# Loading V in key blocks on SP instead of by head on GpSimd, with keys in natural order throughout

## Chip, core and metric

The kernel runs on one core of a Trainium2 chip. The metric is the device time of one execution in microseconds. Six runs of the kernel before have a median of 333.22 us (331.32 to 335.84).

## What is computed

Sliding-window attention over 8 batches of 8 heads, 576 positions and a head size of 64 (a key counts if it is at most 32 positions away), and then, on the 4,608 tokens of 512 features that the heads make side by side, a two-layer block with a squared relu.

```python
scores = scale * np.matmul(q, k.transpose(0, 1, 3, 2))
mask = np.abs(pos[:, None] - pos[None, :]) <= window
attn = softmax(np.where(mask, scores, -1e9))
out = np.matmul(attn, v)
x = out.transpose(0, 2, 1, 3).reshape(B * S, H * D)
h = x @ w_in
g = s * np.maximum(h, 0) ** 2 + b
result = g @ w_out
```

All inputs and the result are float32 in HBM. The kernel works in bfloat16 with float32 sums.

## The kernel before

Two heads make a pair, so there are four pairs. A batch has nine tiles of 64 keys and five units of up to 128 query rows, which lie 32 rows off the tiles. K of a pair is laid out block-diagonally (KBD: head 0 on partitions 0 to 63 and columns 0 to 63, head 1 on the other half of both), so one matmul scores 64 keys of both heads; keys of head 0 stand on the upper half of the score partitions, those of head 1 on the lower. V has the same form (VBD, two slots, one for even and one for odd batches): for a tile of 64 keys, head 0's rows lie on partitions 0 to 63, head 1's on 64 to 127, with two columns of ones for the row sums.

For a unit, TensorE makes the scores (L548) in PSUM (SC, two banks), ACT takes the exponential (L565), DVE multiplies by the 0/1 mask of the window (L571; for batch 0 TensorE adds a mask of large negative numbers instead, L554), TensorE multiplies by V (L588), DVE divides by the row sums (L598, L601), and the rows are transposed into XT, which the two-layer block reads: by TensorE and ACT for batches 0 to 2 (L610, L613), by a DMA transpose on SP after that (L618).

The two-layer block goes over blocks of tokens (128, 128, 256 and then 512). The first layer (function s1) has matmuls L702 into two PSUM banks W, a relu on ACT (L709) and a square on DVE (L711). The second layer (s2) has matmuls L721 into two banks O, an eviction with scale and offset on DVE (L734) and a store on SP (L738). The offset needs column sums of w_out: two sets of 16 matmuls (L744, function colsum), one for each half of w_out's columns.

Loads: q and k come in chunks of 256, 256 and 64 positions with all heads, issued by SP, cast to bfloat16 and transposed (batches 0 and 1: TensorE, L478; from batch 2 on: a DMA transpose on SP, L519, and then for K four DVE copies into KBD, L526). Weights come in 512 KB pieces (L417) and are cast by POOL, ACT or DVE (L420). V comes by head into a single float32 buffer VST and is cast into VBD by four instructions (cast_v, L450 on ACT, L451 on the others). For batches 0 and 1 SP issues eight transfers of 147 KB, one for each head (L437). From batch 2 on POOL issues sixteen transfers of 74 KB, two for each head: positions with an even number go to one 32-partition group, odd ones to the next. With that, the keys of a tile stand evens first, then odds, in V and K from batch 2 on, and the plain K copies L526 write 32 neighbouring columns; for batches 0 and 1 keys are in natural order and the K copies from PSUM (L495, L496) write every second column. So there are two masks: MASKH for natural order and MASK (four equal copies) for evens first.

What orders the work: each instruction is a task with a cost, a key and its data dependences, and a planner builds five queues (TensorE, ACT, DVE, POOL, SP) by simulating them: the task that can start first goes next, and the key decides between equals. Every queue is in order on the chip, so a waiting instruction holds all behind it. Keys count up from −200 for the start-up loads (nxt) and come from the due time of a unit after that. Loads of q and k from batch 2 on wait for an earlier unit's V matmuls (PACE, through paced), and so do those of V (PACEV). A slack tells the planner to plan a reader later than the landing it expects: 3,000 ns for V casts of batches 2 to 7.

Of the kernel before, what the change touches and what calls it, by code (L numbers as in the profile page):

```python
# [22 lines left out]
PACE = ((0, 0, 1, 2, 3, 3), (0, 0, 1, 2, 3, 3), (0, 1, 2, 3, 3, 3))  # L23
PACEV = ((0, 0, 1, 1), (0, 0, 1, 1), (0, 1, 2, 2))
# [4 lines left out]
class _Task:  # L29
    __slots__ = ("n", "stream", "fns", "cost", "lat", "key", "deps", "users", "left",  # L30
                 "ready", "start", "fin", "dma", "sem", "seq", "val", "used", "snap", "slack")

    def __init__(self, n, stream, fns, cost, lat, key, dma, slack):
        self.slack = slack
        self.n, self.stream, self.fns, self.cost, self.lat, self.key, self.dma = \
            n, stream, fns, cost, lat, key, dma
        self.deps, self.users = set(), []
        self.ready = self.start = self.fin = 0.0
        self.sem = self.seq = self.val = None
        self.used = False  # L40
        self.snap = None


class _Graph:
# [7 lines left out]
    def __init__(self, queues):  # L52
        self.queues = queues
        self.tasks = []
        self.writer, self.readers = {}, {}

    def add(self, stream, fns, cost, reads=(), writes=(), key=0.0, accum=False, dma=None, waits=(),
            lat=None, slack=0.0):
        if not isinstance(fns, list):
            fns = [fns]  # L60
        t = _Task(len(self.tasks), stream, fns, cost, self.LAT[stream] if lat is None else lat, key,
                  dma, slack)
        t.deps.update(waits)
        for r in reads:
            assert r in self.writer, r
            t.deps.add(self.writer[r])
        for w in writes:
            if w in self.writer:
                t.deps.add(self.writer[w])
            if not accum:  # L70
                t.deps.update(self.readers.get(w, ()))
        t.deps.discard(t)
        for r in reads:
            self.readers.setdefault(r, []).append(t)
        for w in writes:
            self.writer[w] = t
            if not accum:
                self.readers[w] = []
        self.tasks.append(t)
        return t  # L80
# [33 lines left out]
    def _order(self):  # L114
        free = {s: 600.0 for s in self.STREAMS}
        for t in self.tasks:
            t.left = len(t.deps)
            t.users, t.ready = [], 0.0
# [5 lines left out]
        while len(order) < len(self.tasks):  # L124
            best = None
            for s in self.STREAMS:
                for t in open_[s]:
                    c = (max(free[s], t.ready), t.key, t.n)
                    if best is None or c < best[0]:
                        best = (c, t)  # L130
            assert best is not None, "a cycle"
            (st, _, _), t = best
            open_[t.stream].remove(t)
            t.start = st
            free[t.stream] = st + t.cost
            t.fin = st + t.cost
            if t.dma is not None:
                t.fin = st + self.land.get(t.n, t.cost + 1800.0 + t.dma[1] * t.dma[2])
            order.append(t)
            for u in t.users:  # L140
                u.left -= 1
                if u.stream == "pe" and t.stream == "pe":
                    r = t.fin
                elif t.dma is not None:
                    r = t.fin + 100.0 + u.slack
                elif u.stream == t.stream:
                    r = t.fin + 60.0
                else:
                    r = t.fin + t.lat + (self.MARGIN if u.stream == "pe" else 0.0)
                u.ready = max(u.ready, r)  # L150
                if u.left == 0:
                    open_[u.stream].append(u)
# [85 lines left out]
def bass_sliding_window_symmetric__then__act_starrelu_kernel(  # L238
# [22 lines left out]
    with ExitStack() as es:  # L261
# [19 lines left out]
        VST = sb((128, NTILE, NPAIR, D), F32, "vst")  # L281
# [3 lines left out]
        MASK = sb((128, 4, 128), BF16, "mask")  # L285
# [73 lines left out]
        for p0 in (0, 32, 64, 96):  # L359
            band(MASK[p0:p0 + 32, 0, :], ONESW[p0:p0 + 32, :], ("MASKH", 1, p0),  # L360
                 p0 // 32 % 2, 64 + p0 // 32 % 2, -50, step=2)
# [9 lines left out]
        for i in range(2):  # L371
            for p0 in (0, 64):
                c0 = 64 - p0
                eng = "dve" if i == 0 else "pool"
                key = -97.0 if i == 0 else -1.0
# [8 lines left out]
        for i in range(NEX):  # L384
            for c0 in (0, 192):
                zero("dve", EXO[i][:, :, c0:c0 + 64], ("EXZ", i, c0), 220, key=-96 + i)
        add("dve", lambda e: e.tensor_copy(MASK[:, 1:4, :], MASK[:, 0:1, :].to_broadcast((128, 3, 128))),
            350, reads=[("MASKH", 1, p0) for p0 in (0, 32, 64, 96)], writes=["MASK"], key=-40)
        for pr in range(NPAIR):
# [3 lines left out]
                200, reads=[("MASKH", 0, p0) for p0 in (0, 64)], writes=[("MASKB", pr)], key=-70)  # L393
# [12 lines left out]
        def load_weights(which, i, x, key, eng):  # L406
# [6 lines left out]
            else:  # L413
# [8 lines left out]
                key=key + 20.0, slack=100.0)  # L422
# [5 lines left out]
        def load_v(b, h, key, stream, waits=()):  # L428

            p0 = 64 * (h % 2)  # L430
            for i in range(1 if b < 2 else 2):
                if b < 2:
                    dst, src = VST[p0:p0 + 64, :, h // 2, :], v[b, h, :, :].rearrange("(t p) d -> p t d", p=64)
                else:
                    dst = VST[p0 + 32 * i:p0 + 32 * i + 32, :, h // 2, :]
                    src = v[b, h, i:S - 1 + i:2, :].rearrange("(t p) d -> p t d", p=32)
                add(stream, lambda e, dst=dst, src=src: e.dma_start(dst, src),  # L437
                    640.0 if stream == "sp" else 700.0, writes=[("VST", h, x) for x in (range(2) if b < 2 else [i])],
                    key=key, dma=("v", 1.125, 370.0) if stream == "pool" else ("l", 36, 21.0), waits=waits)
            land["v", b, h] = g.tasks[-1]  # L440

        def cast_v(b, key, engines, slack):
            slot = b % 2
            for x, (a0, a1) in enumerate(((0, 4), (4, 9))):
                for p0 in (0, 64):
                    eng = engines[x][p0 // 64]
                    dst = VBD[slot][p0:p0 + 64, a0:a1, :, p0:p0 + 64].rearrange("p t a c -> p (t a) c")
                    src = VST[p0:p0 + 64, a0:a1, :, :].rearrange("p t a c -> p (t a) c")
                    n = (a1 - a0) * 256
                    add(eng, (lambda e, dst=dst, src=src: e.copy(dst, src)) if eng == "act" else  # L450
                        (lambda e, dst=dst, src=src: e.tensor_copy(dst, src)),  # L451
                        {"act": 190 + 0.833 * n, "dve": 110 + 0.53 * n, "pool": 100 + 1.2 * n}[eng],
                        reads=[("VST", h, i) for h in range(p0 // 64, H, 2) for i in (0, 1)] + [("VBDZ", slot, p0)],
                        writes=[("V", slot, p0, x)], key=key + 0.1 * x, slack=slack)
# [46 lines left out]
        def chunk(b, t0, n, key):  # L501
# [22 lines left out]
            for i in range(2):  # L524
                for p0 in (0, 64):
                    add("dve", lambda e, i=i, p0=p0: e.tensor_copy(  # L526
                        KBD[p0:p0 + 64, :, j0:j0 + nj, p0 + 32 * i:p0 + 32 * i + 32],
# [11 lines left out]
        def unit(b, m):  # L539
# [5 lines left out]
            for j in tiles:  # L545
# [22 lines left out]
                if b > 0:  # L568
                    mask = MASK[:, :, c0:c0 + w] if b > 1 else MASKH[:, c0:c0 + w].rearrange(
                        "p (one c) -> p one c", one=1).to_broadcast((128, 4, w))  # L570
                    add("dve", lambda e, dst=dst, mask=mask: e.tensor_tensor(dst, dst, mask, ALU.mult),  # L571
                        130 + 0.53 * 4 * w, reads=[("E", ei, par)] + (["MASK"] if b > 1 else [("MASKH", 0, p0) for p0 in (0, 64)]), writes=[("E", ei, par)], key=key)
# [7 lines left out]
            for pr in range(NPAIR):  # L580
# [10 lines left out]
            vx = {int(j > 3) for j in tiles} | ({int(2 * m - 1 > 3)} if m > 0 else set())  # L591
            add("pe", fns, len(fns) * 57.0,
                reads=[("E", ei, j % 2) for j in tiles] + ([("E", pi, 1), ("EXZ", pi, 192)] if m > 0 else [])
                + [("EXZ", ei, 0), ("EXZ", ei, 192)] + [("V", slot, p0, x) for p0 in (0, 64) for x in vx]
# [30 lines left out]
        def attention():  # L625
# [20 lines left out]
            qk(0, 0, 128)  # L646
            qk(0, 256, 128)
            for h in range(H):
                load_v(0, h, nxt(), "sp")
            qk(0, 512, 32)  # L650
            cast_v(0, -55.0, (("dve", "act"), ("dve", "pool")), 300.0)
# [8 lines left out]
            qk(1, 0, 128)  # L660
            for h in range(H):
                load_v(1, h, nxt(), "sp", waits=[land["out", 2, 0]])
            cast_v(1, due(1, 0) - 4.0, (("dve", "act"), ("dve", "act")), 800.0)
            qk(1, 256, 128)
            qk(1, 512, 32)
# [5 lines left out]
            for b in range(2, B):  # L671
                for h in range(H):
                    load_v(b, h, due(b, 0) - 30.0 + 0.1 * h, "pool", waits=[paced(b, PACEV[min(b, 4) - 2][h // 2])])
                cast_v(b, due(b, 0) - 4.0, (("dve", "act"), ("dve", "act")), 3000.0)
                for t0, n in ((0, 128), (256, 128), (512, 32)):
                    chunk(b, t0, n, due(b, max(0, t0 // 128 - 1)) - 20.0)
                    for m in {0: (0,), 256: (1, 2), 512: (3, 4)}[t0]:
# [169 lines left out]
```

The softmax here doesn't subtract the row's maximum and nothing guards it: scores larger than these inputs give would overflow.

## Time and profile before

| what | value |
|---|---|
| time of the profiled execution | 333.24 us |
| its span, first to last instruction | 331.5 us |
| TensorE (PE) busy | 308.4 us, 93% |
| VectorE (DVE) busy | 208.8 us, 63% |
| ScalarE (ACT) busy | 162.5 us, 49% |
| GpSimd (POOL) busy | 87.0 us, of which 59.1 for 96 issues of V transfers |
| moved by DMA | 56.56 MB, 171 GB/s on average |
| granted TensorE clock, mean | 0.995 |
| K copies L526, 64x512 and 64x128 | 48 of 287 ns and 24 of 195 ns |
| V casts on DVE, 64x1024 and 64x1280 | 8 of 680 ns and 8 of 810 ns |
| V casts on ACT, 64x1024 and 64x1280 | 8 of 1042 ns and 7 of 1252 ns |

The profile is of one execution, which took 333.24 us; 1.7 us of it lie around the span. Rows of instruction groups give the line, engine, operation and tiles, busy time in all and the mean of one. In the view of waits a row tells which engine and line stood idle, and what ended that. The chain of waits follows the end of the run back from each instruction to what released it; its rows have a start, a length and what it was. A row of the timeline has a start and a length in us, the engine and line, and in brackets the idle time before it and what ended that. The profile's second part has one digit for each fortieth of the span, the busy tenths.

### The profile page before, as it was taken

The page shows a single profiled execution, that of the slowest core. Times are in us where ns is not written, and L with a number is a line of the kernel's source. Part 1 is how long each engine was busy: PE and PEld are TensorE (multiplying, and loading weights), DVE is VectorE, ACT ScalarE, POOL GpSimd, SP SyncE. Part 2 cuts the span into 40 slices and gives each one's busy share as a digit, 9 for nine tenths or more (in the row PEclk, how much of TensorE's full clock was granted, in tenths as well). Part 3 has the DMA queues.
Part 4 walks back from the last instruction along what each step waited for, and adds up shares of the span by engine and source line. Part 5 has one row for each costly group of instructions (what it writes and reads, how often), then busy time and mean ns, then how long its engine had stood idle before and what let it go on. Part 6 is the DMA issues. An engine that isn't in the chain of part 4 may idle for free.

```text
span 331.5 us, 5903 instructions
## 1 busy us (share of the span) xinstructions
PE 308.4 (93%) x2245; PEld 179.1 (54%) x2245; DVE 208.8 (63%) x494; ACT 162.5 (49%) x275; POOL 87.0 (26%) x136
## 2 busy tenths in 40 slices
PE   1687899696999999999999999999999999999995
PEld 1467798664565565446545654565455544444442
DVE  6564788555786797669677858876776453333321
ACT  6686397254563484257326636542664433333300
POOL 8562331940190038003801450253000000000000
PEclk9999999999899999999999999999999999999999
DMA  8999999999399759967998999499932121100022
GB/s 208 228 368 352 256 218 279 285 152 159 86 258 260 137 134 217 204 149 222 241 230 156 237 203 222 116 214 225 232 55 61 50 59 45 50 32 34 32 82 78
DMA packets 105372, 56.56 MB, mean 171 GB/s; under 512 B 54144, under 2 KB 97664, under 8 KB 105344
## 3 DMA queue, kind: packets, MB, share of 16 engines
q1 hardware_dynamic: 100736, 49.10, 65.3%
q0 software_dynamic: 4608, 7.08, 10.6%
q8 instruction: 17, 0.28, 0.4%
q14 instruction: 11, 0.09, 0.1%
HBM read 36.70 MB, written 9.44 MB: 139 GB/s over the span
## 4 chain that ended last, share of the span: by engine, by line
PE 77%; DMA 11%; SPq 4%; POOL 3%; DVE 1%; ACT 1%; issue 1%
PE o L721 34%; PE w L702 33%; DMA stg<-in_moe_w_out_dram 6%; PE avn L588 5%; PE sc L548 4%; DMA vst<-in_v_dram 3%; SPq L437 2%; POOL vst L437 2%; DMA stg<-in_moe_w_in_dram 2%; SPq L461 2%; POOL wout L420 1%; ACT r L709 1%; PE o L744 1%; DVE gt L711 0%; SPq L417 0%
## 5 line engine op out<-in xcount | busy, mean ns | idle before, releaser
L702 PE MATMUL w<-xt,win 128*128 128x512 bf16 (+2 forms) x704 | 143.5, 343 | 2.7 <-ACT r L709 2.7
L721 PE MATMUL o<-wout,gt 128*128 128x512 bf16 (+1 forms) x640 | 141.0, 358 | 1.0 <-POOL wout L420 1.0
L709 ACT ACTIVATE r<-w 128x512 bf16<-128x512 f32 x144 | 85.8, 598 | 93.7 <-PE w L702 80.2
L711 DVE TENSOR_TENSOR gt<-r 128x512 bf16<-128x512 bf16 x144 | 62.0, 440 | 57.4 <-ACT r L709 56.3
L702 PEld LDWEIGHTS w<-xt,win 128*128 128x128 bf16 x704 | 62.4, 98 | 55.4 <-ACT r L709 3.0
L721 PEld LDWEIGHTS o<-wout,gt 128*128 128x128 bf16 x640 | 60.8, 98 | 58.3 <-POOL wout L420 1.3
L437 POOL DMA_DIRECT2D vst<-in_v_dram x96 | 59.1, 624 | 108.1 <-PE sc L548 63.0
L734 DVE SCALAR_TENSOR_TENSOR outs<-o,sb,cvec 128x512 f32<-128x512 f32 (+1 forms) x40 | 27.7, 692 | 18.6 <-PE o L721 17.1
L450 ACT CAST vbd<-vst 64x1024 bf16<-64x1024 f32 (+1 forms) x15 | 16.6, 1140 | 26.6 <-DMA vst<-in_v_dram 26.5
L565 ACT ACTIVATE exe<-sc 128x512 bf16<-128x512 f32 (+1 forms) x40 | 22.2, 554 | 10.9 <-PE sc L548 10.6
L588 PE MATMUL avn<-vbd,exo 128*128 128x130 bf16 (+1 forms) x224 | 25.9, 220 | 1.6 <-ACT xt L613 1.6
L548 PE MATMUL sc<-qt,kbd 128*128 128x128 bf16 (+1 forms) x288 | 25.1, 221 | 0.1
L548 PEld LDWEIGHTS sc<-qt,kbd 128*128 128x128 bf16 x288 | 20.2, 101 | 9.0 <-issue 0.9
L601 DVE TENSOR_TENSOR xn<-avn,rec 128x512 bf16<-128x512 f32 (+1 forms) x36 | 24.6, 683 | 0.3
L588 PE MATMUL avn<-vbd,exe 128*128 128x130 bf16 (+1 forms) x144 | 23.6, 219 | 0.5 <-ACT vbd L450 0.5
L511 DVE CAST nat<-stg 128x1024 bf16<-128x1024 f32 (+1 forms) x36 | 23.9, 678 | 0.1
L588 PEld LDWEIGHTS avn<-vbd,exo 128*128 128x128 bf16 (+1 forms) x224 | 20.6, 104 | 4.4 <-ACT xt L613 1.8
L565 ACT ACTIVATE exo<-sc 128x512 bf16<-128x512 f32 x32 | 19.2, 600 | 2.0 <-PE sc L548 2.0
L526 DVE COPY kbd<-kt 64x512 bf16<-64x512 bf16 (+1 forms) x72 | 18.5, 257 | 0.9
L588 PEld LDWEIGHTS avn<-vbd,exe 128*128 128x128 bf16 (+1 forms) x144 | 15.3, 109 | 3.2 <-ACT vbd L450 0.6
L451 DVE CAST vbd<-vst 64x1024 bf16<-64x1024 f32 (+1 forms) x16 | 11.5, 745 | 7.7 <-DMA vst<-in_v_dram 7.7
L598 DVE RECIPROCAL rec<-avn 128x8 f32<-128x8 f32 (+1 forms) x36 | 7.3, 204 | 12.8 <-PE avn L588 12.6
(74 smaller groups left out, 149.7 us busy)
## 6 DMA issues: line engine op xcount, KB each, us to landing
stg<-in_q_dram SPq DMA_DIRECT2D x16, 512.0 KB, 5.6
stg<-in_k_dram SPq DMA_DIRECT2D x16, 512.0 KB, 7.2
out_dram<-outs SPq DMA_DIRECT2D x32, 256.0 KB, 2.2
vst<-in_v_dram POOLq DMA_DIRECT2D x96, 72.0 KB, 5.8
stg<-in_moe_w_in_dram SPq DMA_DIRECT2D x8, 512.0 KB, 8.6
stg<-in_moe_w_out_dram SPq DMA_DIRECT2D x8, 512.0 KB, 8.8
vst<-in_v_dram SPq DMA_DIRECT2D x16, 144.0 KB, 4.5
stg<-in_q_dram SPq DMA_DIRECT2D x8, 128.0 KB, 7.4
```

What stands on the lines that cost most here:

```text
L437: add(stream, lambda e, dst=dst, src=src: e.dma_start(dst, src), 640.0 if stream == "sp" else 700.0, writes=[("VST", h, x) for x in (range ...
L511: add("dve", lambda e, si=si, ni=ni: e.tensor_copy(NAT[ni][0:n, :, :].rearrange("p i (h d) -> p h i d", h=H), STG[si][0:n, 0:1024].rearran ...
L526: add("dve", lambda e, i=i, p0=p0: e.tensor_copy(KBD[p0:p0 + 64, :, j0:j0 + nj, p0 + 32 * i:p0 + 32 * i + 32], KT[p0:p0 + 64, i, :, t0 // ...
L548: fns = [lambda e, j=j, pr=pr, lo=lo, hi=hi, w=w, par=par: e.matmul(SC[:, par, pr * 128:pr * 128 + w], lhsT=KBD[:, pr, j, :], rhs=QT[slot] ...
L565: add("act", lambda e, src=src, dst=dst: e.activation(dst.rearrange("p a (c i) -> p a c i", i=2), src, AF.Exp, bias=0.0, scale=0.125), 190 ...
L588: fns.append(lambda e, pr=pr, buf=buf, col=col, j=j, x=x, last=len(parts) - 1: e.matmul(av[0:nr, pr, 0:130], lhsT=buf[:, pr, col:col + nr] ...
L601: add("dve", lambda e: e.tensor_tensor(XN[xi][0:nr, :].rearrange("p (a b c) -> p a b c", a=4, b=2), av[0:nr, :, 0:128].rearrange("p a (b c ...
L702: add("pe", [lambda e, g=g, kc=kc: e.matmul(wt[:, g, :], lhsT=WIN_BF[:, kc, (f0 + g) * 128:(f0 + g + 1) * 128], rhs=XT[:, kc, t0 % XR:t0 % ...
L709: add("act", lambda e: e.activation(rt, wt, AF.Relu, bias=0.0, scale=1.0), 190 + 0.833 * 512, reads=[("W", wb)], writes=[("R1", rb)], key=key)
L711: add("dve", lambda e: e.tensor_tensor(GT[gs][:, f0:f0 + ng, g0:g0 + nt], rt, rt, ALU.mult), 130 + 0.53 * 512, reads=[("R1", rb)], writes= ...
L721: add("pe", [lambda e, fc=fc: e.matmul(O[:, ob, 0:cn], lhsT=GT[gs][:, fc, g0:g0 + 128], rhs=WOUT_BF[:, fc, c0:c0 + cn], start=(fc == 0), s ...
L734: add("dve", lambda e: e.scalar_tensor_tensor(OUTS[us][:, 0:cn], O[:, ob, 0:cn], SB128[:, 0:1], CVEC[:, c0:c0 + cn], ALU.mult, ALU.add), 2 ...
```

## The change

V is now issued by SP for all batches, in blocks of 128 positions of all heads (five a batch, the last with 64), into a buffer VST with position on the partitions. A block holds an even tile on partitions 0 to 63 and an odd tile on 64 to 127; the casts move each tile and head to the half of VBD's partitions where the head belongs. There are ten cast instructions a batch instead of four, in three groups (blocks 0 and 1, blocks 2 and 3, block 4), each group behind its q and k chunk. Keys are in natural order for all batches: MASK goes, and the K copies L526 write every second column. Loads of a key under −100 (the start-up's) are bound into one chain, so SP issues them in the order in which the program makes them: q, k and V of a chunk, and then the next chunk. PACE and PACEV have new values, and weight casts and set-up steps have new keys.

```diff
-PACE = ((0, 0, 1, 2, 3, 3), (0, 0, 1, 2, 3, 3), (0, 1, 2, 3, 3, 3))
-PACEV = ((0, 0, 1, 1), (0, 0, 1, 1), (0, 1, 2, 2))
+PACE = ((-1,-1,0,0,1,1),(0,0,1,1,2,2),(0,0,1,1,2,2))
+PACEV = ((-1,-1,0,0,1),(0,0,1,1,2),(0,0,1,1,2))
+EV0 = ("dve", "act", "dve", "pool")
+EV1 = ("dve", "act", "dve", "act")
+EV2 = ("dve", "act", "dve", "act")
...
+        after = [self.chain] if key < -100 and self.chain else []
...
-            t.left = len(t.deps)
+            t.left = len(t.deps) + len(t.after)
...
-        VST = sb((128, NTILE, NPAIR, D), F32, "vst")
+        VST = sb((128, NUNIT, H, D), F32, "vst")
...
-                key=key + 20.0, slack=100.0)
+                key=key + 150.0, slack=100.0)
...
-        def load_v(b, h, key, stream, waits=()):
-
-            p0 = 64 * (h % 2)
-            for i in range(1 if b < 2 else 2):
...
+        def load_v(b, t, key, waits=()):
+
+            n = min(128, S - 128 * t)
+            add("sp", lambda e: e.dma_start(VST[0:n, t, :, :], v[b, :, 128 * t:128 * t + n, :].rearrange("h p d -> p h d")),
+                640.0, writes=[("VST", t)], key=key, dma=("l", n // 2, 18.0), waits=waits)
+            land["v", b, t] = g.tasks[-1]
+
+        VPART = ((0, 2), (2, 4), (4, 5))
+
+        def cast_v(b, x, key, engines, slack):
+
             slot = b % 2
...
+            t0, t1 = VPART[x]
+            for i, (odd, hp) in enumerate(((0, 0), (0, 1), (1, 0), (1, 1))[:4 if x < 2 else 2]):
+                dst = VBD[slot][64 * hp:64 * hp + 64, 2 * t0 + odd:2 * t1 - 1 + odd:2, :, 64 * hp:64 * hp + 64]
+                src = VST[64 * odd:64 * odd + 64, t0:t1, hp::2, :]
+                eng, n = engines[i], (t1 - t0) * 256
...
-                        KBD[p0:p0 + 64, :, j0:j0 + nj, p0 + 32 * i:p0 + 32 * i + 32],
+                        KBD[p0:p0 + 64, :, j0:j0 + nj, p0 + i:p0 + i + 63:2],
...
-                    mask = MASK[:, :, c0:c0 + w] if b > 1 else MASKH[:, c0:c0 + w].rearrange(
-                        "p (one c) -> p one c", one=1).to_broadcast((128, 4, w))
+                    mask = MASKH[:, c0:c0 + w].rearrange("p (one c) -> p one c", one=1).to_broadcast((128, 4, w))
...
-            qk(0, 0, 128)
-            qk(0, 256, 128)
-            for h in range(H):
-                load_v(0, h, nxt(), "sp")
-            qk(0, 512, 32)
-            cast_v(0, -55.0, (("dve", "act"), ("dve", "pool")), 300.0)
+            for x, (t0, n) in enumerate(((0, 128), (256, 128), (512, 32))):
+                qk(0, t0, n)
+                for t in range(*VPART[x]):
+                    load_v(0, t, nxt())
+                cast_v(0, x, -55.0 + x, EV0, 300.0)
...
             for b in range(2, B):
-                for h in range(H):
-                    load_v(b, h, due(b, 0) - 30.0 + 0.1 * h, "pool", waits=[paced(b, PACEV[min(b, 4) - 2][h // 2])])
-                cast_v(b, due(b, 0) - 4.0, (("dve", "act"), ("dve", "act")), 3000.0)
-                for t0, n in ((0, 128), (256, 128), (512, 32)):
+                for x, (t0, n) in enumerate(((0, 128), (256, 128), (512, 32))):
                     chunk(b, t0, n, due(b, max(0, t0 // 128 - 1)) - 20.0)
+                    for t in range(*VPART[x]):
+                        load_v(b, t, due(b, max(0, t0 // 128 - 1)) - 39.9, waits=[paced(b, PACEV[min(b, 4) - 2][t])])
+                    cast_v(b, x, due(b, max(0, t0 // 128 - 1)) - 4.0, EV2, 3000.0)
```

Batch 1 is loaded and cast as batch 0 is (with EV1).

## The prediction

> **What bounds the kernel now.** I read the occupancy row first, then TensorE's waits, then the chain of waits, then the orders of DVE, ACT and TensorE around the holes. The page's second part:
>
> ```profile
> PE   1687899696999999999999999999999999999995
> ...
> DVE  6564788555786797669677858876776453333321
> ...
> DMA  8999999999399759967998999499932121100022
> ```
>
> A slice is 8.29 us. TensorE (PE) is full from slice 11 on; all its holes lie before 83 us. Busy 308.4 of 331.5 us leaves 23.1 us: a start-up without data, two later holes, and 3.4 us of tail behind the last matmul at 328.12. The later holes among TensorE's waits:
>
> ```profile
> PE w L702 <- ACT r L709: 2.7, 1, 2.7
> PE o L744 <- POOL wout L420: 2.7, 1, 2.7
> ```
>
> The chain of waits says what ended them (start, length, what):
>
> ```profile
> 50.92 6.69 DMA stg<-in_moe_w_out_dram
> 57.61 0.05 issue
> 57.67 1.18 POOL wout L420
> 58.85 0.05 POOL vst L437
> 58.90 0.64 issue
> 59.54 1.05 POOL wout L420
> 60.59 7.18 POOL vst L437 x12
> 67.77 10.82 DMA vst<-in_v_dram
> 78.59 0.02 issue
> 78.61 1.42 DVE vbd L451 x2
> 80.03 0.67 DVE gt L711 x2
> ```
>
> So the second column sum (L744, starts 60.65) waits for the last w_out half: data, then POOL's cast. POOL then issues 16 V transfers for batch 2; they land at 78.6, and the V casts stand at the head of two in-order queues:
>
> ```profile
> 78.61 1.42 DVE L451 CAST vbd<-vst 64x1024 bf16<-64x1024 f32 x2 [4.14 <-DMA vst<-in_v_dram]
> ...
> 79.17 2.20 ACT L450 CAST vbd<-vst 64x1024 bf16<-64x1024 f32 x2 [3.60 <-DMA vst<-in_v_dram]
> ...
> 82.04 3.05 PE L702 MATMUL w<-xt,win 128*128 128x512 bf16 x8 [2.75 <-ACT r L709]
> ```
>
> Behind them wait the relu (L709) and square (L711) that free TensorE's two w banks, so TensorE stands 2.75 us. It then restarts slowly: those 8 matmuls take 3.05 us, against 1.73 us for eight of the same kind later. The hole costs 2.75 + 1.32 = 4.07 us.
>
> **What the Trainium skill says.** "Vector Engine (DVE) Microarchitecture Reference", section 5.1: a one-source SBUF copy with 2-byte types takes four elements a cycle if the innermost step is one; without that it still takes two. The trace agrees with the first (64x512 in 287 ns, 64x128 in 195 ns) and shows no strided SBUF copy of that size. "DMA: Bandwidth & Descriptors", "Queues, rings and completion order": an engine takes descriptors of one queue in ring order and alternates between queues; SP owns one queue. Now V of batches 2 to 7 is on POOL's queue beside SP's. During that overlap (70 to 78 us) only 120 to 139 GB/s move, against 349 at 30 to 34 us. "TensorE: Matmul & The Clock Gate", Part 1: after an idle window the clock falls to half. The trace agrees: granted clock 0.58 in 82 to 86 us.
>
> **The method.** From the start of the second column sum (60.65) to the last matmul (328.12), TensorE has that one hole. So end moves by: (shift of the column sum's start) + (matmuls that the new order puts behind it instead of ahead) + (new holes) − 4.07.
>
> **The change, part by part.**
> *Moved matmuls.* The listing of both instruction orders has the same matmuls in all. Ahead of the second column sum the new order has fewer: 4 transposes of xn (0.17 us), 4 of L721 (0.44), 8 of L548 (0.44), 12 of L588 (0.68), durations from the chain's rows. +1.73 us behind it.
> *POOL.* It loses all 96 V issues (59.1 us). One, with its wait, lies between the last two w_out casts: the cast starts at 59.54 without a DMA wait, and the one before ends at 58.71. Gain between 0 and 0.8; I take 0.7.
> *V data of batches 0 and 1.* Eight transfers over half the partitions become five blocks, in pieces of 256 bytes as before, 1.18 MB a batch, all ahead of the last w_out. Now: k of chunk 1 landed at 10.73 and k of chunk 2 at 17.7 (ends of DVE's waits); 0.26 MB of those 7 us are q and k. Three q/k loads of 0.52 MB landed between 5.0 and 10.73, 275 GB/s; so V took 6.0 us (196 GB/s). Bounds for a block: q/k's bandwidth (4.3 us, −1.7) and q/k's time per piece, 1.9 us per 1,024 (8.6 us, +2.6). Since pieces and bytes are the same I take near no change, −0.4 a batch for fewer issues and all partitions: −0.8.
> Shift of the column sum: −0.7 − 0.8 = −1.5. What the new V order gives batch 0's first unit ends in this wait, because w_out's arrival sets it.
> *The 4.07 us hole.* V of batch 2 now goes on SP between the q and k loads, starting right behind w_out; at 255 GB/s (5.1 MB of loads between q of batch 1 at 38.8 and the last w_out near 58.8) all 3.5 MB are in at about 72 us, before the 78.6 of now. The hole goes: −4.07.
> *New holes.* Batch 2's first V cast now stands on DVE and ACT between the last masks of batch 1 and the evictions of second-layer blocks (L734). q, V, k, V (1.57 MB) behind w_out land near 64 to 65 us; DVE is there at about 65. I allow 0.7, between 0 and 3.
> *DVE.* K copies (L526) get a destination step of two. From the V cast rows (680 ns for 1024, 810 for 1280: 0.508 ns an element plus 160) a two-a-cycle copy of 512 takes 420 and of 128 225: 48 x 133 + 24 x 30 = 7.1 us. V casts go from 680 + 810 to 4 x 420 + 290 a batch: +0.48, 3.8 us in eight. Most falls in 90 to 250 us, where DVE is busy 120.65 of 160 us and TensorE 160 of 160: 81% after, hidden under TensorE; 10 us if that cover went. At one element a cycle (the PSUM copies L496 of 512 take 0.70 us) it would be 22 us.
> *ACT.* Casts from 1042 + 1252 to 4 x 622 + 412 a batch: +0.6, hidden: ACT is half idle.
> *Masks.* The plain mask is read as a broadcast, as batch 1 does now (exo 414 ns against 420): nothing. Eight selects on POOL (2.3 us) and a copy (0.35) go, at a time when POOL waits for data anyway.
> *SP.* 24 more issues in all, 0.4 to 0.6 each as for q/k; some 12 us of a queue that waits 63 us for L734 alone. The transposes and stores behind them are rivals B and C.
>
> Sum: −1.5 + 1.73 + 0.7 − 4.07 = −3.1. The profiled execution took 333.24 (span 331.5 and 1.7 around it), as the median of 333.22: 330.1 us.
>
> **Rivals.**
> *A, as summed*, chance 0.42, its own range 327.5 to 332.5.
> *B, the wait is replaced*, 0.23: SP's new order has every q, k and V load of batch 2 ahead of its first DMA transpose (L519), in one queue. With loads in at 72 and 1.25 us a transpose, the first kt is in near 74.5, its K copies done at 76.5; TensorE wants the first scores of batch 2 after 19.2 us of matmuls behind the column sum, 78.4. A rate 15% lower eats that: 2.5 us of hole, 332.6. For it: transposes of 4.1 us at 66 to 79 us now. Against: those ran beside POOL's V.
> *C, slower*, 0.22: from batch 3 on the order on SP is q, k, V, V and then the transpose that writes xt (L618): 1.57 MB ahead of it in the ring instead of one load of 0.52. At the 193 GB/s of 90 to 250 us that is 8.1 us against 2.7, so xt lands 5 us later than now (median 4.9 from issue). It decides once a block's xt has less than that in hand when s1 wants it; with 1.5 us of hole in each of batches 3 to 7, 337.6. For: DMA share 0.94 there. Against: TensorE shows no hole there although V landings kept ACT waiting up to 7.9 us; units run up to 1,024 tokens ahead.
> *D, V blocks as quick as q/k*, 0.13: −3.4 instead of −0.8 and no new hole: 326.8.
>
> **The numbers.** About 1% (3.3 us) is what this measurement tells from no change. The bound 329.9 cuts A: 0.57 of it at most faster, the rest within. Faster: 0.24 from A, 0.13 from D, 0.01 from B = 0.38. Slower: C and 0.02 of B, 0.24. Same: 0.38. Eight in ten: 326.5 (D, also V's lower bound) to 337 (most of C).
>
> **What would show it.** Right: no V wait on DVE or ACT at 75 to 82 us and clock 1.0 there; the column sum (L743 in the new kernel) starting near 59, after a longer wait than 2.7; K copies near 420 ns with TensorE full from 90 us on. Wrong: holes before the first scores of batch 2 (B) or before w matmuls with xt last (C); K copies near 0.7 us with DVE over 90% busy; V blocks much off 1.3 us each; a second clock drop behind the longer wait of the column sum.

## The result, and the profile after

The changed kernel takes 334.35 us (median of 29 runs, 332.01 to 336.86), the kernel before 332.27 us in the same comparison (66 runs). The ratio is 1.0067, 95% interval 1.0049 to 1.0086: slower by 2.2 us (1.6 to 2.9), where 3.1 us less than before had been forecast. Ratios leave out executions over 1.5% above the fastest of their kernel. The two profiled executions do not show this difference: both have a span of 331.5 us (333.24 us before, 333.23 after), since one lies 1 us above its median and the other 1.1 below. The traces tell where time went and came from; how much it is, the repeated runs tell.

The page of the kernel after, second part, in the rows shown of before and with the granted clock:

```profile
PE   1689798989999999999989999999999999999996
...
DVE  7574569979977986697797887678754453233321
...
PEclk9979999999999999999999999999999999999999
DMA  8999999995897799799868994999211120100012
```

The weak slice at 75 to 83 us (the tenth digit, a 6 before) is now a 9. TensorE has an 8 at 66 to 75 and another as late as 166 to 174 us, where it was full, and the clock has its one drop in the start-up (17 to 25 us). Its waits, the rows that matter behind the start-up:

```profile
PE sc L550 <- DVE kbd L528: 2.2, 2, 1.3
...
PE o L720 <- DVE outs L733: 0.8, 2, 0.5
...
PE o L743 <- POOL wout L427: 0.4, 1, 0.4
```

The wait for ScalarE's relu (2.7 us) is gone, and the one of the column sum (now L743) fell from 2.7 to 0.4. New are waits for the K copies (now L528) and for the evictions (now L733). The chain of waits ahead of the column sum:

```profile
49.73 6.49 DMA stg<-in_moe_w_out_dram
56.22 0.05 issue
56.28 1.15 POOL wout L427
...
57.88 1.07 POOLq L787
58.95 0.14 issue
59.09 1.91 PE o L743 x16
```

It starts at 59.09 instead of 60.65. Between 61 and the last matmul TensorE then stands idle five times, 0.46, 0.38, 0.87, 0.19 and 1.29 us, 3.19 in sum. How the longest of them comes about is best read on three engines. SP's queue (the engine column SPq is SP issuing a transfer), from the timeline (start, length, what):

```profile
149.09 0.58 SPq L508 DMA_DIRECT2D stg<-in_q_dram  x1
149.71 0.58 SPq L508 DMA_DIRECT2D stg<-in_k_dram  x1
150.33 2.88 SPq L438 DMA_DIRECT2D vst<-in_v_dram  x2
153.25 3.72 SPq L619 DMA_TRANSPOSE xt<-xn  x1
```

VectorE, and TensorE behind it:

```profile
146.49 0.69 DVE L602 TENSOR_TENSOR xn<-avn,rec 128x512 bf16<-128x512 f32 x1
...
151.45 0.69 DVE L602 TENSOR_TENSOR xn<-avn,rec 128x512 bf16<-128x512 f32 x1 [0.99 <-DMA xt<-xn]
...
158.80 0.69 DVE L602 TENSOR_TENSOR xn<-avn,rec 128x512 bf16<-128x512 f32 x1 [2.01 <-DMA xt<-xn]
...
164.24 0.69 DVE L602 TENSOR_TENSOR xn<-avn,rec 96x512 bf16<-96x512 f32 x1 [0.72 <-DMA xt<-xn]
164.85 1.82 DVE L528 COPY kbd<-kt 64x512 bf16<-64x512 bf16 x4
```

```profile
166.72 0.57 PE L550 MATMUL sc<-qt,kbd 128*128 128x96 bf16 x8 [1.29 <-DVE kbd L528]
```

q, k and two V blocks (1.57 MB) are let in together, and the transpose that empties an xn buffer goes behind them: the rows are written by 147.18, the transpose is issued at 153.25 and has landed at 158.8. So 6.1 us pass before the issue, while SP issues without a pause, and 5.5 behind it. There are two xn buffers, so VectorE can't write the next rows and stands, three times, 3.7 us in all. Its queue is in order, so the K copies behind it start at 164.85, and TensorE's scores wait for them. TensorE never waits for xt itself. The gaps at 71.4 and 72.4 us have the same form with the output buffers: VectorE stands 1.95 us for a store that SP issued behind two V blocks.

### The profile page after: what moved, and what is told of

Its sections match the earlier page's. It is cut to its first block, busy times and chain, and to the rows that moved or that the text cites. A ratio compares the mean times of both kernels' runs of the same rounds, so it can differ in the third digit from the quotient of the medians.

```text
span 331.5 us, 5838 instructions
## 1 busy us (share of the span) xinstructions
PE 309.5 (93%) x2245; PEld 179.8 (54%) x2245; DVE 220.7 (67%) x517; ACT 168.3 (51%) x298; POOL 24.8 (7%) x33
## 4 chain that ended last, share of the span: by engine, by line
PE 74%; DMA 11%; DVE 8%; ACT 3%; issue 2%; SPq 0%; POOL 0%; POOLq 0%; DVEq 0%
PE w L701 31%; PE o L720 30%; DMA stg<-in_moe_w_out_dram 6%; PE avn L589 5%; PE sc L550 4%; DMA xt<-xn 3%; DMA out_dram<-outs 2%; DVE kbd L528 2%; DVE outs L733 1%; PE o L743 1%; DVE gt L710 1%; ACT r L708 1%; DVE maskb L397 1%; DVE vbd L352 1%; PE sc L556 1%
## 5 line engine op out<-in xcount | busy, mean ns | idle before, releaser
L720 PE MATMUL o<-wout,gt 128*128 128x512 bf16 (+1 forms) x640 | 144.0, 358 | 3.5 <-DVE wout L427 1.5
L710 DVE TENSOR_TENSOR gt<-r 128x512 bf16<-128x512 bf16 x144 | 60.2, 426 | 51.0 <-ACT r L708 50.2
L733 DVE SCALAR_TENSOR_TENSOR outs<-o,sb,cvec 128x512 f32<-128x512 f32 (+1 forms) x40 | 27.7, 692 | 15.9 <-PE o L720 12.4
L528 DVE COPY kbd<-kt 64x512 bf16<-64x512 bf16 (+1 forms) x72 | 27.1, 376 | 0.8
L550 PEld LDWEIGHTS sc<-qt,kbd 128*128 128x128 bf16 x288 | 20.5, 101 | 11.9 <-DVE kbd L528 3.1
L452 ACT CAST vbd<-vst 64x512 bf16<-64x512 f32 (+1 forms) x38 | 21.7, 571 | 6.8 <-DMA vst<-in_v_dram 6.2
L572 DVE TENSOR_TENSOR exe<-exe,maskh 128x512 bf16<-128x512 bf16 (+1 forms) x35 | 14.5, 416 | 5.8 <-ACT exe L567 5.6
L453 DVE CAST vbd<-vst 64x512 bf16<-64x512 f32 (+1 forms) x40 | 16.3, 407 | 1.4 <-DMA vst<-in_v_dram 1.1
```

The costliest lines, as they stand in the source:

```text
L528: add("dve", lambda e, i=i, p0=p0: e.tensor_copy(KBD[p0:p0 + 64, :, j0:j0 + nj, p0 + i:p0 + i + 63:2], KT[p0:p0 + 64, i, :, t0 // 2:t0 // ...
L550: fns = [lambda e, j=j, pr=pr, lo=lo, hi=hi, w=w, par=par: e.matmul(SC[:, par, pr * 128:pr * 128 + w], lhsT=KBD[:, pr, j, :], rhs=QT[slot] ...
L710: add("dve", lambda e: e.tensor_tensor(GT[gs][:, f0:f0 + ng, g0:g0 + nt], rt, rt, ALU.mult), 130 + 0.53 * 512, reads=[("R1", rb)], writes= ...
L720: add("pe", [lambda e, fc=fc: e.matmul(O[:, ob, 0:cn], lhsT=GT[gs][:, fc, g0:g0 + 128], rhs=WOUT_BF[:, fc, c0:c0 + cn], start=(fc == 0), s ...
L733: add("dve", lambda e: e.scalar_tensor_tensor(OUTS[us][:, 0:cn], O[:, ob, 0:cn], SB128[:, 0:1], CVEC[:, c0:c0 + cn], ALU.mult, ALU.add), 2 ...
```

## The experiments

Three theories stood at first. T: the forecast gain came, and VectorE gave it back, because its added work meets late transfers. R1: the strided K copies alone cost it. R2: transposes and stores stand behind V in SP's queue.

**Stride alone, in the kernel before** (e1; keys from batch 2 on then stand in wrong columns).

```diff
-KBD[p0:p0 + 64, :, j0:j0 + nj, p0 + 32 * i:p0 + 32 * i + 32]
+KBD[p0:p0 + 64, :, j0:j0 + nj, p0 + i:p0 + i + 63:2]
```

> The kernel before with one edit: the K copies L526 write every second column as in the changed kernel (keys of batches 2 to 7 then stand in the wrong columns of K for their V and mask). The order of instructions stays. Each 64x512 copy should go from 287 to about 447 ns, the 64x128 ones from 195 to 233, 8.6 us more on DVE in all. Theory T (the changed kernel lost its gain partly to this DVE time, but only where DVE also stands for late transfers): hidden here, at most +0.3% (333.3). Rival R1 (the stride alone gave the gain back): +2 to +4 us, 334.3 to 336.3. Rival R2 (only the shared ring matters): no change.

Measured: 1.0122 (1.007 to 1.0174). In the order of before the stride costs about 4 us (2.3 to 5.8): it is not hidden, though TensorE was full there. T and R2 missed here, and R1 had this run right. New gaps at 93.6 (mask), 208 and 239 us (relu) came beside the old hole.

**The change without the stride** (e2: the edit above the other way, in the kernel after; keys misplaced likewise).

> The changed kernel with its K copies L528 writing 32 neighbouring columns again (keys of batches 2 to 7 then stand in the wrong columns for V and mask); order of instructions unchanged. T: copies back at about 287 ns, the holes before the scores at 141 and 167 us (0.87 and 1.29 us) shrink to nearly nothing, -2 us of 334.35, so about 332.3, ratio to before 1.000. R1: -4 us or more, 330.3, ratio 0.994. R2: holes stay since the late transposes make them, ratio 1.005 to 1.007.

Measured: 1.0048 (1.0019 to 1.0076). R1's 0.994 and T's 1.000 both lie outside: without the stride 1.6 of the 2.2 us are still there. As the interval overlaps that of after, what the stride costs in this order is not told from nothing. VectorE still stood 5.8 us for xt (5.7 in after) and 5.1 us for stores (3.4).

**A quarter of V** (e3: V of batches 2 to 7 loads 2 of 8 heads, the rest is stale).

```diff
+            hn = 8 if b < 2 else 2
-VST[0:n, t, :, :], v[b, :, ...]
+VST[0:n, t, 0:hn, :], v[b, 0:hn, ...]
```

> The changed kernel with V of batches 2 to 7 loaded for two of the eight heads only (the rest of the buffer keeps the values of earlier batches, which the casts read as before): three quarters of V's bytes leave SP's ring, every instruction stays. R2 (transposes and stores late behind V in the one ring): DVE's waits for xt transposes and stores (5.7 and 3.4 us) go and with them most holes behind 60 us: -3 to -4 us, 330.5 to 331.3, ratio 0.995 to 0.997. T: about -2 us, ratio 1.000. R1: no change, ratio 1.005 to 1.007.

Measured: 0.9921 (0.9899 to 0.9943), 329.07 us, faster than any of the three theories had it. Behind the column sum TensorE has no gap left, and VectorE waits for no transpose and no store, with the strided copies in place and VectorE as busy (221.8 us). So with a quarter of V VectorE's longer busy time costs TensorE nothing in this order; that it can in another, e1 shows.

**More buffers** (e4: `NXN` 2 to 3, `NOUT` 3 to 4), and the same in the kernel before as a control (e7).

> The changed kernel with three xn buffers instead of two and four outs buffers instead of three, bytes and ring as they are; the planner may move a few instructions. DVE then need not stand for the xt transpose (five waits, 5.7 us) or the store (two waits, 3.4 us). R2 by way of these buffers: the holes at 71 to 72 us (0.84) and 141 and 167 us (2.2) go: -2 to -3 us, ratio 0.998 to 1.001. T: about -2 us. R1: no change, 1.005 to 1.007.

> Control for the run of after with more buffers: the kernel before with the same third xn and fourth outs buffer. If those buffers cured what the change brought in (transposes and stores behind V in SP's ring), they are worth nothing here: ratio 0.997 to 1.003, 331.5 to 333.3 us, since before shows no long wait of DVE for xt or for the stores. If they help any version alike, the ratio is about 0.995, 330.6 us, and the 1.7 us that they gave the kernel after say nothing about the change.

Measured: 1.0017 (0.9994 to 1.0041) after, 1.0028 (1.0002 to 1.0054) before. The buffers give the kernel after 0.5% and the one before nothing, so they cure something that the change brought in. They don't cure all of it: in e4's trace VectorE stands only 0.4 us for xt and never for a store, but three gaps of TensorE are left, 2.0 us, each a few us after VectorE has stood for K or V.

**Queue or bytes** (e5: V of batches 2 to 7 on GpSimd's queue; e10: order as in after, SP's V as light as in e3, and GpSimd's queue loads the other six heads at the same times into a buffer that nobody reads).

```diff
+            if b > 1:
+                add("pool", lambda e: e.dma_start(SCR[0:n, t % 3, :, :], v[b, 2:8, ...]),
+                    700.0, writes=[("SCR", t % 3)], key=key, dma=("v", 1e-5, 1.0), waits=waits)
```

> The kernel after with the V blocks of batches 2 to 7 issued by GpSimd on its own queue instead of SP; same bytes, same blocks of 128 keys of all heads, same casts, strided K copies kept. R2 (what costs is that the xt transposes, the output stores and q and k stand behind V in SP's queue): DVE's waits of xn for xt and of outs for the store fall from 5.7 and 5.1 us to under 1 us each, the TensorE holes at 71 to 73 and at 166.7 us go, and the time falls by 2 to 5 us, to 329.5 to 332.5 us, ratio 0.985 to 0.995. If instead V's bytes themselves load the DMA engines, whichever queue they are in: the same waits stay within 1 us of what they are, and the time stays at 333.5 to 335 us. T and R1 (DVE's own time, the strided K copies): within 0.4% of after, ratio 1.003 to 1.010, since no copy changes. GpSimd's issue stands on its queue behind the r casts, so a wait of V casts for V may come back as it was in before (26 us on ScalarE); that would leave the time between the two.

> The kernel after in the same order on TensorE, VectorE, ScalarE and SP, with SP's V loads of batches 2 to 7 bringing 2 of 8 heads as in the run that measured 0.992, while GpSimd's own queue loads the other 6 heads at the same times into a buffer that nobody reads (part of V is left stale). The same bytes move as in after; SP's queue is as light as in the 2-head run. If the loss came from standing behind V in SP's queue: as the 2-head run, ratio 0.990 to 0.995, no DVE wait for xt over 1 us. If V's bytes at the DMA engines made it, whatever queue they are in: as after, ratio 1.004 to 1.010, xt and outs waits of 3 us and more. Between the two, 0.997 to 1.003: both. T and R1 expect no difference from the 2-head run, since no copy on VectorE changes.

Measured: e5 1.0289 (1.0238 to 1.0341), far slower than anything expected; the planner also ordered all engines anew, so only e10 tells the two apart: 1.0103 (1.008 to 1.0127), as after or a little slower, and not as e3. VectorE's waits in e10:

```profile
DVE xn L607 <- DMA xt<-xn: 4.8, 5, 1.5
...
DVE outs L738 <- DMA out_dram<-outs: 1.0, 1, 1.0
```

R2 falls in its plain form. With SP's queue as light as in e3, the same bytes in another queue bring the waits for transposes back (4.8 us against 5.7 in after and none in e3), those for stores less so (1.0 against 3.4). That is what the Trainium skill says ("DMA: Bandwidth & Descriptors", "Issuing engines are not separate DMA queues": transfers of all issuers run on the same engines and interleave). SP's own issues slow down with them: 28 V blocks between 59 and 250 us took SP 34 us in e10, 25.5 in e3 with the same small blocks, and 37 in after. Of the 5.1 us between the spans of e3 and e10, 1.9 lie ahead of the column sum (60.03 against 61.91; the granted clock is 0.57 from 56 to 60 us in e10 and 1.00 in e3, so they need not come from V) and 2.8 behind it, up to the last matmul. After has 4.3 us more than e3 there, so a part of the loss may still be SP's queue; one trace of each doesn't tell.

**V later** (e11, e12: both buffers, and V's planned time 39.9 us ahead of its unit made 20 and 30; q and k unchanged).

> The kernel after with the third xn and the fourth outs buffer, and with the V blocks' planned time 20 us later than in after, so that in SP's queue most V blocks of batches 3 to 7 stand apart and behind the transposes instead of in pairs ahead of them. Computes the whole. If order in SP's queue is what costs: 1 to 3 us less than after with the buffers alone, 330 to 332 us, ratio 0.993 to 0.999, faster than both kernels. If V then comes late for its casts: waits of ScalarE and VectorE for V of 5 us and more, ratio 1.003 to 1.015. If the bytes make it: as with the buffers alone, ratio 1.000 to 1.004.

> As the run before it with the V blocks' planned time 10 us later instead of 20. If order in SP's queue is what costs, and V's casts have more room: 0.994 to 1.000. If the bytes make it: 1.000 to 1.004.

Measured: 1.0033 (1.0007 to 1.0059) and 1.0073 (1.005 to 1.0096). No gain over the buffers alone (e4, 1.0017): with V later, ScalarE stands 9.9 us for V in e11, against 5.1 in e4.

**The price of the hole** (e6: V of batch 2 on SP in the kernel before; e9: before in its own order, but V of batch 2 brings 2 of 9 tiles, so the rest is stale).

```diff
+                if b == 2:
+                    dst, src = dst[:, 0:2], src[:, 0:2]
```

> The kernel before with only the V loads of batch 2 moved from GpSimd's queue to SP's (by head, as before; the casts, the K order and the order of the rest as the planner gives it). It tests the price of the hole at 79.3 to 82 us in the sum of the prediction (2.75 us idle and 1.32 us of slow clock). If that price holds and nothing is given back: hole gone, time 4.07 us lower, 328.2 us, ratio 0.988. If the hole was worth only its idle time: 329.5 us, ratio 0.992. If it was cover for work that is late anyway, or V in SP's ring makes the transposes of batch 2 late: 331.5 to 333.5 us, ratio 0.998 to 1.004, with new holes between 82 and 110 us.

> The kernel before, every instruction in its old order on every engine, except that GpSimd's 16 V loads of batch 2 bring only 2 of 9 tiles each (16 KB instead of 72 KB; the rest of V of batch 2 is left stale). V of batch 2 then lands early, so this takes away the hole at 79.3 to 82 us alone. If the price in the prediction holds (2.75 us idle and 1.32 us of slow clock, nothing given back): 4.07 us less, ratio 0.987 to 0.989, 328 us. If only the idle time counts: ratio 0.991. If what TensorE does after the hole is held by something else anyway, as the run with V of batch 2 in SP's queue (1.017, a new hole of 3.6 us one batch later) may say: ratio 0.996 to 1.004, with new holes after 82 us.

Measured: e6 1.0171 (1.0124 to 1.0217). The hole at 79 to 82 us goes, and a longer one comes one batch later, again behind V casts that wait for GpSimd's V:

```profile
109.85 0.26 PE L588 MATMUL avn<-vbd,exo 128*96 128x130 bf16 x1 [3.62 <-ACT xt L613]
```

The planner had ordered the rest anew, so e6 prices nothing. e9 does: 0.9944 (0.9922 to 0.9966), 1.9 us (1.1 to 2.6) instead of 4.07. In its profiled execution the slow clock came elsewhere:

```profile
61.52 3.47 PE L746 MATMUL o<-wout,onesw 128*128 128x256 bf16 x16 [2.39 <-POOL wout L420]
```

The 16 matmuls of the column sum took 3.47 us there against 1.92. The clock drop that the forecast booked on the hole is not bound to it.

**The start-up** (e8: GpSimd's second zeroing of VBD[1], a memset, moved behind w_in; e13: V of batch 1 behind all q and k of batch 1; e14: e13 with the buffers).

> The kernel after with GpSimd's second zeroing of the second block-diagonal V buffer put behind the arrival of w_in, so that it no longer runs beside VectorE's four mask rows at 5.7 to 8.0 us. If that memset is what slowed them: the mask rows' mean falls from 1102 to 250 to 350 ns, the first scores start at 10.5 to 11 us instead of 12.16, and TensorE then waits 1 to 2 us more before the second column sum, which is set by w_out's arrival at 59 us: time 333.5 to 335 us, ratio 1.004 to 1.009, no gain. If the start-up's 1.5 us reach the end: 332.8 us, ratio 1.002. If something else slowed the mask rows: they stay at about 1100 ns.

> The kernel after with V of batch 1 loaded behind all six q and k pieces of batch 1 instead of between them (computes the whole). If V ahead of the last q and k piece is what makes TensorE late at 52 to 55 us: its waits for GpSimd's and VectorE's nat casts there fall from 0.9 to 2 us to under 0.3 us, the column sum waits 1 to 3 us for w_out again and starts at 58.5 to 60 us, and the time falls by 0.5 to 1.5 us, ratio 1.002 to 1.006. If the start-up is not part of the loss: as after, 1.005 to 1.010.

> e13 with the third xn and the fourth outs buffer, which gave after 0.5%. If both losses add up: ratio 0.997 to 1.001. If one covers the other: 1.001 to 1.005.

Measured: e8 1.0078 (1.0047 to 1.011). The four operations that write the mask maskb (now L398) fell to 254 ns in the median, the first scores came at 10.49 us instead of 12.16, and nothing reached the end. e13 1.0222 (1.0188 to 1.0256) and e14 1.0201 (1.0179 to 1.0224): a clear miss of both expectations. The waits for GpSimd's q and k cast went, and VectorE stood 10.3 us for xt in e13. (Its column sum comes at 63.41 us, but with 48 more matmuls ahead of it than in after, as in the fast e16 at 63.90.) Why this order of the start is so much worse with the pacing of after is not settled; with that of before it costs nothing (e16).

**Pacing** (e15: both buffers and the pacing of before for q and k, V's five blocks alike; e16: e15 with e13's edit; e17: e15 without the buffers; e18: e15 with V's table as in after).

```diff
-PACE = ((-1,-1,0,0,1,1),(0,0,1,1,2,2),(0,0,1,1,2,2))
-PACEV = ((-1,-1,0,0,1),(0,0,1,1,2),(0,0,1,1,2))
+PACE = ((0, 0, 1, 2, 3, 3), (0, 0, 1, 2, 3, 3), (0, 1, 2, 3, 3, 3))
+PACEV = ((0,0,1,1,1),(0,0,1,1,1),(0,1,1,2,2))
```

> The kernel after with both buffers and with the pacing tables of before for q and k (and V's five blocks let in at units 0, 0, 1, 1, 1 and, from batch 4, 0, 1, 1, 2, 2). If letting V, q and k in earlier is what made them meet the transposes and stores: ratio 0.993 to 0.999, 330 to 331.7 us. If it is the bytes at any time, or VectorE's own time: as after with the buffers alone, 0.999 to 1.005. If q, k and V now come late for their casts: 1.006 and more, with new waits of VectorE and ScalarE for stg and vst.

> e15 with V of batch 1 behind all q and k of batch 1, the version that both theories of what is left would favour: 0.990 to 0.997 if both hold, 0.999 to 1.005 if neither does.

> The kernel after with the pacing of before for q and k and V's blocks at 0, 0, 1, 1, 1 and 0, 1, 1, 2, 2, no buffer added. If the early pacing is the cause, and the buffers were only its first victims: ratio 0.993 to 0.999, holes behind the column sum under 1 us in sum, no VectorE wait for xt over 1 us. If both pacing and buffers are needed: 0.999 to 1.005, with waits for xt and the stores left.

> The kernel after with both buffers and the pacing of before for q and k alone; V's table stays that of after. If q and k early are what collides: as e15, 0.993 to 0.998. If V early is: as the buffers alone, 1.000 to 1.004.

Measured: e15 0.9955 (0.9934 to 0.9975), e16 0.9947 (0.993 to 0.9964), e17 1.0029 (1.0005 to 1.0052), e18 0.9982 (0.9945 to 1.0019). e15 and e16 beat both kernels, with the whole computed and the strided copies kept. In e15 TensorE is full behind the column sum:

```profile
PE   1669798999999999999999999999999999999995
...
DMA  8999899999799699889979996899512111000021
```

The same stretch of SP's queue as above, in e15:

```profile
143.65 2.25 SPq L619 DMA_TRANSPOSE xt<-xn  x1
145.94 0.57 SPq L508 DMA_DIRECT2D stg<-in_k_dram  x1
146.55 1.94 SPq L438 DMA_DIRECT2D vst<-in_v_dram  x2
148.54 2.38 SPq L619 DMA_TRANSPOSE xt<-xn  x1
```

From batch 4 on q and k of the two large chunks are let in at units 0, 1, 2 and 3 instead of 0, 0, 1 and 1, so less stands ahead of each transpose, and VectorE has no wait for xt or a store left. The pacing alone (e17) missed its better forecast: VectorE still stands 2.2 us for xt and 0.4 for a store, and TensorE has 1.7 us of gaps. The buffers and the pacing each give about 0.4 to 0.5%, together 1.1%. Whether V's own table has a part stays open: e18's interval holds both answers. So does how much is the time at which the loads are let in and how much the order that the planner makes of it, since each table gives a new one.

## Why the prediction was wrong, step by step

- *Shift of the column sum, −1.5.* Right: −1.56 in the pair of traces. In nine executions with after's order on TensorE up to there and its start-up undisturbed it starts at 59.8 on average (57.7 to 62.9), in five of before's order at 61.1 (60.65 to 61.52): −1.25. The forecast had the wait grow, but it shrank, since TensorE itself came later (first scores at 12.16 us instead of 10.71), and the start spreads more.
- *Matmuls put behind it, +1.73.* Right: the order is what the listing said.
- *The hole, −4.07.* The first step that failed, in its size. The mechanism was right (no V wait there, clock 1.0), but the hole was worth 1.9 us in e9 (1.1 to 2.6), 2.2 less than booked. e9's trace has 0.6 us of small new gaps, so 2.1 of the 2.75 us of idle time were saved, and the slow clock stayed. The record has the mean granted clock of each execution: of the 206 of the kernel before that the experiments' ratios use, 53 at 0.998 or more took 331.0 us on average and 124 at 0.993 to 0.997 took 332.0; in e9 these are 329.3 (8) and 330.5 (11). So a lower clock goes with about 1 us, hole or no hole. In the kernel after no such difference shows (334.4 in 10, 333.9 in 10), and its traced drop lies in the start-up; whether the change saved that 1 us and lost it elsewhere stays open.
- *New holes, +0.7 (0 to 3).* The second step that failed, and the one that turned the sign: 3.19 us of idle TensorE in the trace, 2.5 more than booked. With the other terms as measured, −1.25 + 1.73 − 1.9 + 3.2 = +1.8, against 2.2 (1.6 to 2.9) measured. Without new holes the sum is −1.4, and e15, which has none, came 1.6 us below before (331.73 against 330.12). That the sums come out so well is in part luck: they mix single traces with medians, and in the pair of traces itself −1.56 + 1.73 + 3.19 − 4.07 gives −0.7, while the last matmuls end 0.1 us apart (328.11 and 328.22), so 0.8 us is in no term.
- *SP, some 12 us for 24 more issues.* Too small: with the loads in one queue a V issue took 1.33 us (37 us for 28), not 0.4 to 0.6, and the delay of the transposes and stores behind it was left to the rivals.
- *VectorE, hidden under TensorE.* K copies took 447 and 233 ns instead of 420 and 225, VectorE's sum rose by 11.9 us instead of 10.9. That they would be hidden was wrong for the order of before (e1, 4 us); in that of after the cost is not told from nothing (e2). A busy share of 81% was no proof of cover.
- *Rival C* had the order that does the harm: q, k, V, V and then the transpose. It looked only at the last reader of xt, TensorE, with up to 1,024 tokens in hand, and that reader never waited. The one who waited was the writer of the two xn buffers, VectorE. That is about half of it: more buffers (e4) all but end its waits and give 0.5 of the 1.1%. The pacing tables stood in the diff and were given no term of their own; in e15 other tables, with the order that the planner made of them, leave no gap at all.
- *Rivals B and D* did not come: TensorE has no gap before the first scores of batch 2, and the column sum came 1.56 us earlier, not the 4 that quick V blocks would have given.

## What to carry to other kernels

When loads move to another queue, follow each buffer that a transfer empties as well as each that it fills, and ask which in-order engine waits to write it and what stands behind that instruction there. A different queue does not take bytes away; when they are let in did more here, so price the admission table of a change as a change of its own. A hole is worth what a run without it shows, not its idle time plus a slow clock that may come anyway.

## What the runs showed of the hardware

Two of four operations on VectorE took about 2 us beside a memset on GpSimd, and ended just behind it. These are the four that write maskb, first in after, all four and then the last two, and then all four in e8 (operation, count, shortest, median and longest in ns, first and last start):

```profile
L397 DVE TENSOR_SCALAR maskb<-maskh x4: 211/1112/1971, 5.7 to 7.8; 128x128 bf16<-128x128 bf16 x4
L397 DVE TENSOR_SCALAR maskb<-maskh x2: 211/238/266, 7.6 to 7.8; 128x128 bf16<-128x128 bf16 x2
```

```profile
L398 DVE TENSOR_SCALAR maskb<-maskh x4: 163/254/362, 5.7 to 6.1; 128x128 bf16<-128x128 bf16 x4
```

In after a memset of 2,304 elements a partition runs from 5.55 to 7.57 us. The first two operations start at 5.68 and 5.76, take 1.97 and 1.96 us and end at 7.65 and 7.72; the last two, behind it, take 0.27 and 0.21. In e8, with the memset moved away, none takes more than 0.36. The Trainium skill ("GPSIMD Engine Reference", specifications) says that GpSimd shares its SBUF interfaces with VectorE, with contention in some of VectorE's modes; the runs agree and give the size. Which mode these operations ran in, no run shows. A copy of 64x512 in bfloat16 takes 447 ns with a destination step of two, against 287 without.

The fall of TensorE's clock that the prediction cites is not tied to one length of idle time. It came after 2.75 us without a matmul in before (granted clock 0.58 from 82 to 86 us) and with a wait of 2.39 us in e9 (0.54 from 61.5 to 65), but not after 2.70 us in before, ahead of the column sum (1.00 from 60 to 64).
